# Attention and SwiGLU on one core: where the casts of wo stand behind the exponentials, and which places the last projected rows use

## The chip, the cores and the metric

The kernel runs on one core of a Trainium2 chip. The metric is the device time of one execution in microseconds; the time before is the median of three runs. A profiled execution, whose instructions are quoted below, is a run of its own with a time of its own.

## The reference, cut to what matters

```python
S, D, H, Dh, F = 2048, 576, 32, 18, 4608

def A(x, wqkv, w_phi, wo):                    # linear attention with a learned feature map
    q, k, v = heads_of(x @ wqkv)              # 32 heads of 18 columns
    pq, pk = q @ w_phi, k @ w_phi             # per head
    phi_q = concat(softmax(pq), softmax(-pq)) # over the 18 columns of a head
    phi_k = concat(softmax(pk), softmax(-pk))
    kv, z = phi_k^T v, sum_s phi_k            # per head
    o = (phi_q kv) / (phi_q z + 1e-6)
    return o @ wo

def B(x, w_gate, w_up, w_down):
    return (silu(x @ w_gate) * (x @ w_up)) @ w_down

xn = layernorm(x)
out = x + A(xn) * silu(B(xn))
```

All inputs and the output are float32.

## The kernel before, in words

Products are made at float32 accuracy from parts. A helper `split(hi, lo, src)` casts a tile to TensorE's own 32-bit format on ACT (line 58) and subtracts the cast from the source on DVE (line 59); a product is then three matmuls of the parts. `split_rows` (lines 62 to 64) does the same for the weights of the early gate and up tiles.

The program has these stages, in order of time.

1. Layer norm, transposes, and the folding of the feature map into the weights of k and q (to about 100 us).
2. k and v: 16 tiles of 128 rows, and the sums kv and z (to about 230 us).
3. q and the projection (about 230 to 480 us): 16 tiles of 128 rows, two at a time. `q_tile` multiplies the rows by the folded weights into a PSUM tile of one place (`p2`, two banks; in the trace its matmuls write `p`). `softmax_parts` reads that tile on DVE four times (lines 278 and 279, a maximum and a subtraction, then a minimum and a subtraction, into the SBUF tile `e`), then makes two exponentials on ACT in place (line 282) and sums them by heads on DVE (`sm`, line 285). What follows of `q_tile` on DVE is the denominator: `ez` is `e` times z (line 567), `y` its sums (line 569), five small operations (lines 571 to 576), and `e` times the result (line 577). `numer` transposes `e` of a pair of tiles on TensorE (line 588), splits, and multiplies by kv (line 594). `project` multiplies by the parts `WOH` and `WOL` of wo (line 614); ACT copies each half of 128 x 288 out of PSUM into an SBUF tile `so` (line 619), and ACT's own DMA queue stores it (line 620).
4. gate, up and down with Strassen's scheme, two passes of 1024 rows (about 513 us to the end). `gate_up_weights` loads weights into `ld`, makes sums on GpSimd (POOL, lines 694 to 697), splits them into `w`, and stores the parts in DRAM for the second pass. Its first call stands before the loop over the units.

Between and beside stages 2 to 4, "early" tiles of gate and up (`early_tile`) run as plain products: a gate product into a PSUM tile `pe` (two places), a silu of it on ACT into `h` (line 119), an up product into the other place, and a multiplication on DVE (line 122). Their weights come through `raw` in `early_weights`.

`tails(n)` prepares tails of the gate and up weights: a load into `tl`, four POOL subtractions (lines 546 to 549), a cast into `th` on ACT (line 550), a DVE subtraction, and twelve stores that POOL issues.

wo comes in five groups of rows, two groups to a tile: `wrs` lists three tiles, which take the places of `oh`, `ol` and, for the last group, `ez`. `split_wo`, called after the second of the first two q tiles, splits them into `WOH` and `WOL`.

What sets the order: a scheduler places each engine's instructions at compile time, by priority (the order of the program, unless a block is under `tc.high_priority()`) among those that its own times hold ready; each engine then runs its list in that order. `with tc.issue_after(ins)` puts the block's instructions that run on the engine of `ins` behind `ins` in that engine's list, and no others. A pool's tile name with `bufs=n` has n places; a tile that finds none free waits for the release of the oldest. `read` lists the DVE subtractions of `softmax_parts`, so `read[-1]` is a DVE instruction.

Of the kernel before, what the change touches and what calls it, by code (L numbers as in the profile page):

```python
# [9 lines left out]
F32 = mybir.dt.float32  # L10
F32R = mybir.dt.float32r
AF = mybir.ActivationFunctionType
# [4 lines left out]
S, D, H, DH, F = 2048, 576, 32, 18, 4608  # L17
P = 128
# [5 lines left out]
HALF = D // 2  # L24
# [13 lines left out]
def heads(ap):  # L38
    return ap.rearrange("p (h d) -> p h d", d=DH)
# [7 lines left out]
def gated_hedgehog_kernel(ctx: ExitStack, tc, x, w_qk, w_v, w_phi, wo, w_gu, w_tail, w_down, ident_in, mask_in, out):  # L47
# [5 lines left out]
    nc = tc.nc  # L53
# [3 lines left out]
    def split(hi, lo, src):  # L57
        nc.scalar.copy(hi, src)  # L58
        nc.vector.tensor_sub(lo, src, hi)  # L59
# [53 lines left out]
    def early_tile(f, i, parts, js=(0, 1), banks=None):  # L113
        for j in js:
            pg, pu = banks or [eps.tile([P, BT], F32, name="pe") for _ in range(2)]
            xw(pg, i, j, slice(0, BT), *parts[0], False)
            h = epool.tile([P, BT], F32, name="h")
            with tc.high_priority():
                nc.scalar.activation(h, pg, AF.Silu)  # L119
            last = xw(pu, i, j, slice(0, BT), *parts[1], False)  # L120
            with tc.high_priority():
                nc.vector.tensor_mul(h, pu, h)
            nc.sync.dma_start(h_dram[i, f, :, j * BT:(j + 1) * BT], h)
        return last

    with ExitStack() as att:
        const = att.enter_context(tc.tile_pool(name="const", bufs=1))
        ident = const.tile([P, P], F32, name="ident")
# [7 lines left out]
        with ExitStack() as wst:  # L136
# [129 lines left out]
            kk = kst.enter_context(tc.tile_pool(name="kk", bufs=2, side="right", reuse_waits="tile"))  # L266
# [6 lines left out]
            def softmax_parts(ps, e):  # L273
                m = kk_pool.tile([P, 2, H], F32, name="m", bufs=1)
                p4 = ps[:, :, 0:HALF].rearrange("p a (h d) -> p a h d", d=DH)
                for s, op in enumerate((ALU.max, ALU.min)):
                    m3 = m[:, s].rearrange("p (a h) -> p a h", a=2)
                    nc.vector.tensor_reduce(m3, p4, axis=AX.X, op=op)
                    read.append(nc.vector.tensor_sub(e[:, s * D:(s + 1) * D].rearrange("p (a h d) -> p a h d", a=2, d=DH),
                                                     p4, m3.unsqueeze(3).to_broadcast([P, 2, H // 2, DH])))  # L280
                for s in range(2):
                    nc.scalar.activation(e[:, s * D:(s + 1) * D], e[:, s * D:(s + 1) * D], AF.Exp,
                                         scale=1.0 if s == 0 else -1.0)
                sm = kk_pool.tile([P, 2 * H], F32, name="sm")
                nc.vector.reduce_sum(sm, heads(e), axis=AX.X)
                return sm

            kk_pool, read = kk, []

            def kv_step(n, phi, v):  # L290
                for i in range(2 * NG):
# [108 lines left out]
            def k_tile(t):  # L400
                i0, j0, cols = block(t)
                pk = kps.tile([P, 2, 512], F32, name="p2")
                for i in range(2):
                    w = slice(i * HALF, (i + 1) * HALF)
                    xw(pk[:, i, 0:HALF], i0, j0, cols, KVWH[:, :, :, w], KVWL[:, :, :, w], True)
                phi = kk.tile([P, 2 * D], F32, name="phi", bufs=2)
                sm = softmax_parts(pk, phi)
                nc.vector.reciprocal(sm, sm)
                nc.vector.tensor_mul(heads(phi), heads(phi), spread(sm, 2 * H))
                return phi  # L410
# [111 lines left out]
        with ExitStack() as qst:  # L522
            qw = qst.enter_context(tc.tile_pool(name="qw", bufs=1, reuse_waits="tile"))
            qk = qst.enter_context(tc.tile_pool(name="qk", bufs=2, reuse_waits="tile"))
# [1 line left out]
            WOH = qw.tile([GW, NG, D], F32R, name="WOH")  # L526
            WOL = qw.tile([GW, NG, D], F32R, name="WOL")
            wrs = [qk.tile([P, 2, D], F32, name="oh", bufs=1), qk.tile([P, 2, D], F32, name="ol", bufs=1),
                   qk.tile([P, 2, D], F32, name="ez", bufs=1)]
            for g, (o, w) in enumerate(GROUPS):  # L530
                nc.sync.dma_start(wrs[g // 2][0:w, g % 2], wo[o:o + w, :])

            def split_wo():
                with tc.issue_after(read[-1].ins):
                    for n, wr in enumerate(wrs):
                        g, w = slice(2 * n, min(2 * n + 2, NG)), GROUPS[2 * n][1]
                        split(WOH[0:w, g], WOL[0:w, g], wr[0:w, 0:min(2, NG - 2 * n)])

            kk_pool = qk
# [58 lines left out]
            def project(b, oh, ol, last):  # L598
                for j in range(QS // P):
                    pair = qps.tile([P, 2, 512], F32, name="p2") if last and j == 0 else None  # L600
                    jc = slice(j * P, (j + 1) * P)
                    r0 = b * QS + j * P
                    for i in range(2):
                        n = slice(i * HALF, (i + 1) * HALF)
                        if pair:
                            ps = pair[:, i]
                        elif last and i:
                            ps = qps.tile([P, 2, 512], F32, name="p2")[:, 0]
                        else:
                            ps = qps.tile([P, 512], F32, name="p")  # L610
                        k = 0
                        for g, (o, w) in enumerate(GROUPS):
                            for a, bw in ((oh, WOH), (oh, WOL), (ol, WOH)):
                                nc.tensor.matmul(ps[:, 0:HALF], a[0:w, g, jc], bw[0:w, g, n], start=k == 0,  # L614
                                                 stop=k == 3 * NG - 1)
                                k += 1
                        so = qk.tile([P, HALF], F32, name="so", bufs=2)
                        with tc.high_priority() if last else ExitStack():
                            nc.scalar.copy(so, ps[:, 0:HALF])
                        nc.scalar.dma_start(s_dram[r0:r0 + P, n], so)  # L620

            order = list(range(S // QS // 2, S // QS)) + list(range(S // QS // 2))
# [1 line left out]
            for n in range(S // QS + 1):  # L624
                new = []
                if n > 0:
                    om = numer(es)
                if n < S // QS:
                    new += [q_tile(order[n] * (QS // P) + j) for j in range(QS // P)]
                if n == 0:  # L630
                    split_wo()
                if n > 0:
                    project(order[n - 1], *om, n == S // QS)
                es = new
# [34 lines left out]
    def gate_up_weights(i, f):  # L669

        parts, wt = {}, fw.tile([96, 7, P], F32R, name="wt", bufs=2)
        n, q = divmod(f - EARLY, 4)
        if i == 0:
            ld = fw.tile([P, 2, D], F32, name="ld", bufs=2).rearrange("p a b -> p (a b)")
            ld = ld[:, 0:8 * P].rearrange("p (m c n) -> p m c n", m=4, c=2)
            nc.sync.dma_start(ld, w_gu[f, :, :, 0:2])
            ts = fw.tile([P, D], F32, name="ts")[:, 0:4 * P].rearrange("p (m c n) -> p m c n", m=2, c=2)

        def ready(m, src):
            k = 1 if m == 6 else 2  # L680
            w = fw.tile([P, k, 4, P], F32R, name=f"w{k}", bufs=2 if k == 1 else 4)
            if i:
                nc.sync.dma_start(w.bitcast(F32), w_dram[f - EARLY, :, m:m + k])
            else:
                split(w[:, :, 0:2], w[:, :, 2:4], src)
                if f < NF - 1:
                    nc.sync.dma_start(w_dram[f - EARLY, :, m:m + k], w.bitcast(F32))
            for c in range(k):
                parts[m + c] = w[:, c]

        ready(0, None if i else ld[:, 0:2])
        nc.sync.dma_start(wt.bitcast(F32), t_dram[n, q].rearrange("b r m n -> (b r) m n"))
        if i == 0:
            nc.gpsimd.tensor_sub(ts[:, 0], ld[:, 2], ld[:, 0])
            nc.gpsimd.tensor_sub(ts[:, 1], ld[:, 3], ts[:, 0])
            nc.gpsimd.tensor_sub(ld[:, 2], ld[:, 3], ld[:, 2])
            nc.gpsimd.tensor_sub(ld[:, 1], ld[:, 1], ts[:, 1])  # L697
        ready(4, None if i else ts)
        ready(2, None if i else ld[:, 2:4])
        ready(6, None if i else ld[:, 1:2])  # L700
        return parts, wt
# [319 lines left out]
    todo = [(i, f) for i, n, f in units if f >= EARLY and (i == 0 or f < NF - 1)]  # L1021
# [5 lines left out]
        nc.sync.dma_start(t, w_down[f * P:(f + 1) * P, :])  # L1027
    xo = operands(0)
    early_tile(EARLY - 1, 0, parts)
    ready = [gate_up_weights(*todo.pop(0))]  # L1030
    est.close()
    fq = ctx.enter_context(tc.tile_pool(name="fq", bufs=1, reuse_waits="tile"))
    fps = ctx.enter_context(tc.tile_pool(name="fps", bufs=1, space=PSUM, reuse_waits="tile"))
# [72 lines left out]
```

## Time and profile before

| | |
|---|---|
| Median of three runs | 1636.75 us (1635.69, 1636.75, 1640.77) |
| Profiled execution, its own time | 1638.38 us |
| Its span, first to last instruction | 1636.6 us |
| TensorE (PE) busy | 1604.0 us, 98% |
| DVE busy | 1168.5 us, 71% |
| ACT busy | 721.9 us, 44% |
| POOL busy | 653.3 us, 40% |
| Granted TensorE clock, mean | 0.998 of full speed |

PE is the matmul, PEld TensorE's loading of weights, which overlaps it; SP issues most DMAs. In a timeline a row is: start in us from the start of the span, duration in us, engine, line, operation, output tile and input tiles, shape, count, and in brackets the idle time of that engine just before with what ended it. In a table of waits a row is: who waited, for what, total us, times, longest us. Consecutive instructions of one engine overlap a little, so a row can start before the row ahead of it has ended.

### The profile page before, as it was taken

The numbers are of one execution on the slowest core, as the hardware profiler recorded it, in microseconds if no ns is written. First come the engines' busy times: TensorE is split into PE (matmuls) and PEld (weight loads), VectorE is DVE, ScalarE is ACT, GpSimd is POOL, SyncE is SP. The second block draws the span as 40 slices with busy tenths as digits, with TensorE's granted clock in tenths as the row PEclk, the third lists the DMA queues.
The fourth block names the chain that finished last, engine by engine and source line by source line (L and its number), as shares of the span: only waits on it lengthen the run. The fifth ranks groups of instructions, "written<-read, shape, count | busy, mean of one in ns | idle before, by whom it ended". The sixth has DMA issues, their size and how long they took to land.

```text
span 1636.6 us, 25198 instructions
## 1 busy us (share of the span) xinstructions
PE 1604.0 (98%) x9385; PEld 1429.7 (87%) x9385; DVE 1168.5 (71%) x1721; ACT 721.9 (44%) x1391; POOL 653.3 (40%) x699
## 2 busy tenths in 40 slices
PE   6999998999999999999999999999999999999998
PEld 5899997999978888888888888888888888888887
DVE  7677768899952678778777778825666766666578
ACT  5533345444432554544444544455433433333334
POOL 3485661333212455455545355313233324133132
PEclk9999999999999999999999999999999999999999
DMA  9622243334248545555554554684454655555444
GB/s 286 206 80 78 85 134 117 117 103 126 67 144 306 184 165 175 179 178 168 177 180 165 175 192 152 224 296 150 136 162 135 199 184 170 172 179 185 140 115 174
DMA packets 121741, 268.46 MB, mean 164 GB/s; under 512 B 12787, under 2 KB 53363, under 8 KB 119827
## 3 DMA queue, kind: packets, MB, share of 16 engines
q1 hardware_dynamic: 106652, 246.49, 45.9%
q0 software_dynamic: 3072, 11.02, 2.4%
q10 hardware_dynamic: 11894, 9.35, 1.8%
q8 instruction: 74, 1.21, 0.3%
q14 instruction: 49, 0.39, 0.1%
HBM read 167.19 MB, written 99.61 MB: 163 GB/s over the span
## 4 chain that ended last, share of the span: by engine, by line
PE 90%; DMA 4%; DVE 3%; POOL 1%; issue 1%; ACT 1%; SPq 0%; ACTq 0%; POOLq 0%; DVEq 0%
PE px L707 24%; PE pd L832 24%; PE pw L707 12%; PE py L707 6%; PE p L92 6%; PE pe L92 5%; PE p L614 4%; PE po L594 2%; PE kvp L294 2%; PE vx L382 1%; PE pt L588 1%; DMA xn<-in_A_x 1%; PE vw L382 1%; DMA s_dram<-so 1%; DMA sraw<-in_A_w_v 1%
## 5 line engine op out<-in xcount | busy, mean ns | idle before, releaser
L832 PEld LDWEIGHTS pd<-dw,hh 128*128 128x128 f32 x3048 | 432.4, 188 | 26.4 <-DVE dw L59 1.7
L832 PE MATMUL pd<-dw,hh 128*128 128x288 f32 x3048 | 448.5, 297 | 4.3 <-DVE dw L59 1.5
L707 PE MATMUL px<-X,w 128*128 128x512 f32 x1488 | 384.3, 393 | 0.0
L707 PEld LDWEIGHTS px<-X,w 128*128 128x128 f32 x1488 | 270.6, 188 | 51.8 <-ACT s L736 2.0
L707 PE MATMUL pw<-X,w 128*128 128x512 f32 x732 | 188.7, 393 | 0.0
L707 PEld LDWEIGHTS pw<-X,w 128*128 128x128 f32 x732 | 137.0, 188 | 30.5
L741 DVE TENSOR_TENSOR s<-pw,s 128x512 f32<-128x512 f32 x124 | 85.1, 688 | 100.0 <-ACT s L736 89.2
L957 DVE TENSOR_TENSOR acc<-pd,acc 128x576 f32<-128x576 f32 x128 | 96.2, 752 | 83.8 <-PE pd L832 83.6
L736 ACT COPY s<-px 128x512 f32<-128x512 f32 x124 | 72.6, 585 | 157.2 <-PE px L707 157.2
L92 PE MATMUL pe<-X,wh 128*128 128x512 f32 (+1 forms) x380 | 121.8, 401 | 5.8 <-ACT h L119 2.9
L59 DVE TENSOR_TENSOR hh<-ha,hh 128x512 fp32r<-128x512 f32 x140 | 111.5, 823 | 20.7 <-ACT hh L58 19.1
L58 ACT CAST hh<-ha 128x512 fp32r<-128x512 f32 x140 | 82.7, 619 | 92.4 <-PE pd L832 73.5
L929 POOL TENSOR_TENSOR hb<-hb 128x512 f32<-128x512 f32 x34 | 47.0, 1381 | 168.6 <-DVE hb L753 161.4
L59 DVE TENSOR_TENSOR w<-ld,w 128x512 fp32r<-128x512 f32 (+1 forms) x93 | 77.2, 832 | 35.7 <-ACT w L58 34.5
L707 PE MATMUL px<-X,wt 96*128 96x512 f32 x248 | 97.9, 395 | 0.0
L707 PE MATMUL py<-X,w 128*128 128x512 f32 x372 | 96.5, 394 | 0.0
L916 POOL TENSOR_TENSOR h<-ha,hb 128x512 f32<-128x512 f32 x34 | 44.3, 1302 | 126.8 <-DVE ha L757 88.6
L942 POOL TENSOR_TENSOR ha<-ha 128x512 f32<-128x512 f32 x34 | 52.6, 1564 | 103.5 <-DVE hh L59 103.5
L58 ACT CAST w<-ld 128x512 fp32r<-128x512 f32 (+1 forms) x93 | 51.0, 549 | 89.6 <-POOL ld L697 56.8
L92 PEld LDWEIGHTS pe<-X,wh 128*128 128x128 f32 (+1 forms) x380 | 70.0, 189 | 21.7 <-ACT h L119 3.4
L761 ACT COPY py<-px 128x512 f32<-128x512 f32 x62 | 35.5, 572 | 102.7 <-PE px L707 80.8
L707 PEld LDWEIGHTS py<-X,w 128*128 128x128 f32 x372 | 66.7, 188 | 11.2
(262 smaller groups left out, 3199.0 us busy)
## 6 DMA issues: line engine op xcount, KB each, us to landing
w_dram<-w SPq DMA_DIRECT2D x90, 512.0 KB, 2.9
w<-w_dram SPq DMA_DIRECT2D x90, 512.0 KB, 4.5
wt<-t_dram SPq DMA_DIRECT2D x61, 336.0 KB, 3.7
ld<-in_B_w_gu SPq DMA_DIRECT2D x31, 512.0 KB, 4.5
X<-sum_dram SPq DMA_DIRECT2D x8, 1280.0 KB, 11.1
rt<-in_B_w_down SPq DMA_DIRECT2D x33, 288.0 KB, 3.1
rb<-in_B_w_down SPq DMA_DIRECT2D x33, 288.0 KB, 4.7
w_dram<-w SPq DMA_DIRECT2D x30, 256.0 KB, 2.1
```

Source lines behind the costliest of these rows:

```text
L58: nc.scalar.copy(hi, src)
L59: nc.vector.tensor_sub(lo, src, hi)
L92: last = nc.tensor.matmul(ps, l, r, start=n == 0, stop=n == len(pairs) - 1)
L614: nc.tensor.matmul(ps[:, 0:HALF], a[0:w, g, jc], bw[0:w, g, n], start=k == 0, stop=k == 3 * NG - 1)
L707: nc.tensor.matmul(ps, l, r, start=first and n == 0, stop=last and n == len(mm) - 1, skip_group_check=True)
L736: nc.scalar.copy(t, ps)
L741: nc.vector.tensor_add(t, ps, t)
L832: nc.tensor.matmul(ps, l, r, start=first and n == 0 and m == 0, stop=n == len(hs) - 1 and m == 2, skip_group_check=True)
L916: sub(s, g["h"][0][0], g["h"][0][1])
L929: nc.gpsimd.tensor_add(a21, a21, g["h"][1][1])
L942: sub(a12, a12, g["h"][0][0])
L957: nc.vector.tensor_add(a2, pd[:, :, 0:HALF], a2)
```

## The change

- In `softmax_parts` the exponentials are recorded in a new list `exps`. `split_wo` puts its block behind `exps[-1]`, the second exponential of the second q tile, on ACT, instead of behind `read[-1]`, that tile's last subtraction, on DVE.
- The third of the `wrs` tiles takes one of the four places of `e` instead of the one place of `ez`.
- In the last call of `project`, the second half of each row block (`i` = 1) is copied into a place of `e` instead of `so`. All output copies are recorded in a list `outs`.
- The first call of `gate_up_weights` puts its ACT instructions behind `outs[-1]`, the last output copy.

```diff
+    outs = []
...
                 for s in range(2):
-                    nc.scalar.activation(e[:, s * D:(s + 1) * D], e[:, s * D:(s + 1) * D], AF.Exp,
-                                         scale=1.0 if s == 0 else -1.0)
+                    last = nc.scalar.activation(e[:, s * D:(s + 1) * D], e[:, s * D:(s + 1) * D], AF.Exp,
+                                                scale=1.0 if s == 0 else -1.0)
+                exps.append(last)
...
-            kk_pool, read = kk, []
+            kk_pool, read, exps = kk, [], []
...
             wrs = [qk.tile([P, 2, D], F32, name="oh", bufs=1), qk.tile([P, 2, D], F32, name="ol", bufs=1),
-                   qk.tile([P, 2, D], F32, name="ez", bufs=1)]
+                   qk.tile([P, 2 * D], F32, name="e", bufs=4).rearrange("p (a n) -> p a n", a=2)]
...
             def split_wo():
-                with tc.issue_after(read[-1].ins):
+                with tc.issue_after(exps[-1].ins):
...
-                        so = qk.tile([P, HALF], F32, name="so", bufs=2)
+                        if last and i:
+                            so = qk.tile([P, 2 * D], F32, name="e", bufs=4)[:, 0:HALF]
+                        else:
+                            so = qk.tile([P, HALF], F32, name="so", bufs=2)
                         with tc.high_priority() if last else ExitStack():
-                            nc.scalar.copy(so, ps[:, 0:HALF])
+                            outs.append(nc.scalar.copy(so, ps[:, 0:HALF]))
                         nc.scalar.dma_start(s_dram[r0:r0 + P, n], so)
...
-    ready = [gate_up_weights(*todo.pop(0))]
+    with tc.issue_after(outs[-1].ins):
+        ready = [gate_up_weights(*todo.pop(0))]
```

## The prediction

> **What bounds the kernel now.** I read the page's busy times first, then the table of TensorE's waits over the span, then the timelines of PE, ACT and DVE around the two places that the change touches.
>
> ```profile
> PE 1604.0 (98%) x9385; PEld 1429.7 (87%) x9385; DVE 1168.5 (71%) x1721; ACT 721.9 (44%) x1391; POOL 653.3 (40%) x699
> PE tp L193 <- DVE xn L181: 11.4, 2, 10.4
> ```
>
> TensorE is busy for 98% of the span. The change removes no matmul, so it can only give back time in which PE stands still, and 11.4 us of that lie at the start, before anything that the change touches. Around the two places PE stands still six times:
>
> ```profile
> 247.53 0.29 PE L92 MATMUL p<-QH,X 128*128 128x288 f32 x1
> ...
> 255.40 0.50 PE L92 MATMUL pe<-X,wh 128*128 128x512 f32 x1 [1.19 <-ACT h L119]
> 260.49 0.50 PE L92 MATMUL pe<-X,wh 128*128 128x512 f32 x1 [1.55 <-DVE h L122]
> 270.36 0.37 PE L92 MATMUL p<-QH,X 128*128 128x288 f32 x1 [1.42 <-DVE e L279]
> ...
> 477.94 0.40 PE L614 MATMUL p<-WOH,oh 126*128 126x288 f32 x1 [1.17 <-ACT so L619]
> 485.39 0.50 PE L92 MATMUL pe<-X,wh 128*128 128x512 f32 x1 [0.28 <-ACT h L119]
> 489.57 0.47 PE L92 MATMUL pe<-X,wh 128*128 128x512 f32 x1 [0.63 <-ACT h L119]
> ```
>
> The brackets add up to 1.19 + 1.55 + 1.42 = 4.16 us in the first place and 1.17 + 0.28 + 0.63 = 2.08 us in the second: 6.24 us together, the most that the change can return directly. A measurement of this kernel can tell about 0.3%, 4.9 us, from no change, so nearly all of it has to come back before the change counts as faster.
>
> Why PE waits in the first place is seen on ACT and DVE, from the first q tile's exponentials on:
>
> ```profile
> 239.61 1.26 ACT L282 ACTIVATE e<-e 128x576 f32<-128x576 f32 x2
> 244.86 1.16 ACT L58 CAST WOH<-oh 126x1152 fp32r<-126x1152 f32 x1 [3.99 <-DMA oh<-in_A_wo]
> 248.05 1.16 ACT L58 CAST WOH<-ol 126x1152 fp32r<-126x1152 f32 x1 [2.04 <-DMA ol<-in_A_wo]
> 249.12 0.66 ACT L58 CAST WOH<-ez 72x576 fp32r<-72x576 f32 x1
> 251.19 0.94 ACT L550 CAST th<-tl 128x896 fp32r<-128x896 f32 x1 [1.41 <-POOL tl L549]
> 252.04 0.68 ACT L282 ACTIVATE e<-e 128x576 f32<-128x576 f32 x1
> ...
> 253.46 1.28 ACT L119 ACT_TABLE_LOAD   x1
> 254.75 0.60 ACT L119 ACTIVATE h<-pe 128x512 f32<-128x512 f32 x1
> 255.37 1.28 ACT L282 ACT_TABLE_LOAD   x1
> 256.66 0.69 ACT L282 ACTIVATE e<-e 128x576 f32<-128x576 f32 x1
> 257.36 1.28 ACT L119 ACT_TABLE_LOAD   x1
> 258.98 0.60 ACT L119 ACTIVATE h<-pe 128x512 f32<-128x512 f32 x1 [0.33 <-PE pe L92]
> ```
>
> ```profile
> 243.00 1.35 DVE L285 TENSOR_REDUCE sm<-e 128x64 f32<-128x1152 f32 x1
> 244.27 0.75 DVE L278 TENSOR_REDUCE m<-p 128x32 f32<-128x576 f32 x1
> ...
> 246.51 0.76 DVE L279 TENSOR_TENSOR e<-p,m 128x576 f32<-128x576 f32 x1
> 247.19 1.35 DVE L59 TENSOR_TENSOR WOL<-oh,WOH 126x1152 fp32r<-126x1152 f32 x1
> 253.47 0.69 DVE L63 TENSOR_TENSOR wl<-raw,wh 128x512 fp32r<-128x512 f32 x1 [4.94 <-ACT wh L62]
> ...
> 255.90 0.75 DVE L59 TENSOR_TENSOR WOL<-ez,WOH 72x576 fp32r<-72x576 f32 x1
> 257.24 1.34 DVE L567 TENSOR_TENSOR ez<-e,zb 128x1152 f32<-128x1152 f32 x1
> 259.76 0.68 DVE L122 TENSOR_TENSOR h<-pe,h 128x512 f32<-128x512 f32 x1
> 269.46 0.75 DVE L279 TENSOR_TENSOR e<-p,m 128x576 f32<-128x576 f32 x1
> ```
>
> ACT stands with the casts of wo at the head of its list, waiting for their DMAs (3.99 and 2.04 us), then with `th` waiting for POOL (1.41 us). The second q tile's numbers are subtracted by 246.51 + 0.76 = 247.27, yet its exponentials start at 252.04 and 256.66. DVE therefore idles 4.94 us before 253.47, while even the first tile's `ez`, whose exponentials ended at 240.87, cannot run: its only place holds the last wo rows until their subtraction (255.90). It comes at 257.24. From 253.47 on DVE works off a queue, and two of PE's waits, 1.55 and 1.42, are for operations in it (259.76 and 269.46).
>
> In the second place ACT waits twice:
>
> ```profile
> 473.36 0.40 ACT L619 COPY so<-p 128x288 f32<-128x288 f32 x1 [1.02 <-PE p L614]
> 476.97 0.62 ACT L58 CAST w<-ld 128x512 fp32r<-128x512 f32 x1 [3.22 <-DMA ld<-in_B_w_gu]
> 477.50 0.39 ACT L619 COPY so<-p 128x288 f32<-128x288 f32 x1
> 481.18 0.40 ACT L619 COPY so<-p 128x288 f32<-128x288 f32 x1 [3.29 <-DMA s_dram<-so]
> 483.92 0.40 ACT L619 COPY so<-p 128x288 f32<-128x288 f32 x1 [0.26 <-DMA s_dram<-so]
> 484.74 0.60 ACT L119 ACTIVATE h<-pe 128x512 f32<-128x512 f32 x1
> ```
>
> The second of the last four copies stands behind a cast of `w` that waits 3.22 us for its load, and PE waits for the bank that it frees. The third waits 3.29 us for the first one's store, because there are two `so` places; the silu at 484.74, for which PE waits 0.28, stands behind it.
>
> **The change part by part.**
>
> *Casts of wo behind the second tile's exponentials.* Nothing is added; three casts (1.16 + 1.16 + 0.66 = 2.98 us on ACT) and their subtractions move. The exponentials can run from 247.27, and the casts follow with their DMAs landed: 247.3 + 1.4 + 3.0 = 251.7 for the end of them, about where `th` stands now. WOL is read first at 277.0, so the casts have 20 us of cover:
>
> ```profile
> L614 PE MATMUL p<-WOL,oh x160: 289/294/299, 277.0 to 479.8; 126*128 126x288 f32 x128, 72*128 72x288 f32 x32
> L707 PE MATMUL px<-X,w x36: 389/393/405, 512.8 to 528.5; 128*128 128x512 f32 x36
> ```
>
> Queued behind the casts on ACT are `th`, `wh` and the silu of 254.75. One exponential (0.68) no longer lies ahead of that silu, so of the 1.19 us wait I take 0.6; bounds: all 1.19, or a loss of 2.98 if the casts, instead of the idle time, stand ahead of it. With both exponentials together, two table loads (255.37 and 257.36, 2 x 1.28 us) should also go; the waits that follow belong to DVE, so I give that nothing. [...]
>
> *The last wo rows in an `e` place.* Four places, of which the first three q tiles take three and the fourth the freed one; its load is the same. `ez` of the first tile can now run once DVE reaches it, in the idle 4.94 us. DVE then stands nearly 5 us earlier in its queue, and PE's two waits on it add up to 2.97: I take both, 1.55 + 1.42. Bounds: 0, if the hole stays closed, and 2.97. What is late next would be the silu on ACT. First place: 0.6 + 2.97 = 3.57 us.
>
> *Output copies first, two in `e` places.* The `e` places are those of q tiles that `numer` has long transposed, so none of the four copies has a store to wait for. The second copy, at 477.50, can follow the first, at 473.76: the 1.17 goes. The silu is no longer behind copies that wait: the 0.28 goes. Of the 0.63 I take half, 0.3, since the wait is for a second `pe` place too, which a multiplication on DVE frees, and DVE's list there holds subtractions of weights. Second place: 1.75 us; bounds 1.17 and 2.08.
>
> *First gate and up weights behind the last copy.* The new wait: casts of `w` stand behind a copy whose product, fifteen matmuls of at most 0.3 us, starts at 477.94 - 1.17 = 476.8 and ends by 481.3. Four casts of at most 0.62 us end by 483.8, before the silu of today (484.74). Behind them wait POOL's sum into `ld`, SP's stores of `w`, and the loads of `w_down` rows that SP issues after; the first product reads `w` at 512.8, 29 us later. Cost nothing; without that cover, up to the 4.3 us by which the first cast (476.97) moves.
>
> *Sum.* 3.57 + 1.75 = 5.3 us. The profiled execution, 1638.38, would be 1633.1; its time stands 1.6 above the median of the three runs, so the median goes from 1636.75 to 1631.4, 0.32% faster.
>
> **The rivals.**
>
> *`th` takes the casts' place at the head of ACT's list.* The scheduler put `th` ahead of the second tile's exponentials, by its own times, although it comes later in the program; with the casts held back, it has no reason to put it later. ACT then stands until POOL is done (251.19) and the exponentials run at 252.04 and 256.66 as now. The casts follow at 257.35 and end at 260.33; the silu of 258.98 slides to there, and PE's wait at 260.49 grows: 260.33 + 0.60 + 0.68 = 261.6, 1.1 us later. DVE still does the first tile's work in its hole, so the 1.42 goes. Net 0.3, with the second place 2.0 us: 1634.7, no change that can be told. For it speaks the position of `th` today; against it, that `th` was placed when ACT had the casts as company. [...]
>
> *The first tile's denominator goes ahead of the second tile's reads.* `ez` comes earlier in the program than the second tile's maximum (244.27), and it is no longer held. What one tile has from `ez` on takes DVE 5.5 us without a break:
>
> ```profile
> 453.87 1.35 DVE L567 TENSOR_TENSOR ez<-e,zb 128x1152 f32<-128x1152 f32 x1
> ...
> 458.00 1.36 DVE L577 TENSOR_TENSOR e<-e,y 128x1152 f32<-128x1152 f32 x1
> ```
>
> (458.00 + 1.36 - 453.87 = 5.49.) Placed after `sm` (243.00), it moves the reads, and with them PE's next q tile, which needs their bank, from 247.53 to 253.0; the exponentials follow, and then 2.98 us of casts ahead of a silu. If PE's list has nothing in front, it loses 5.5 + 3.0 = 8.5; it gains 1.75 at the end and the 1.42. Net 5.3 slower: 1642.0. It decides from a loss of 8.1 us on (4.9 + 3.2); any early product of 3 us that PE takes in between brings it back to no change. The priorities speak for it; PE's supply of early products speaks against the full price.
>
> *The change doesn't act*: the order is as before, 1636.8.
>
> **How the numbers follow.** Forecast 42%, `th` 36%, the denominator ahead 20%, no effect 2%. So faster by over 0.3%: 0.42; within: 0.38; slower: 0.20. The low end takes all 6.24 us and the 1.1 by which the lowest of the three runs lies under the median: 1629.4. The high end is the slower rival, 1642.0; the range between holds both signs, and the forecast's own range is 1629.4 to 1632.0 (the second place at 1.17 instead of 1.75).
>
> **What would show it.** Right: on ACT both exponentials of the second tile before the first WOH cast and close to 248, no table load between them; on DVE `ez` before 253 and no idle time near 5 us ahead of `wl`; PE without the waits of 1.55 and 1.42; four `so` copies with no DMA in their brackets, and no L614 wait for `so`. Wrong: `th` ahead of the exponentials with a POOL wait of several us; a PE wait for `e` L279 near 247; or new PE waits after 513, where the order of the rest may have shifted.

## The result, and the profile after

The changed kernel takes 1643.63 us (median of 6 runs, 1641.54 to 1645.53); the kernel before, in runs beside it, 1638.09 us. The ratio is 1.0034, with a 95% interval of 1.002 to 1.0047: slower by 0.34%, where 1631.4 us, 0.32% faster, was forecast, and above the range's high end of 1642.0. The profiled execution of after took 1641.54 us, the lowest of the six, span 1639.4. Lines below 126 keep their numbers; in `softmax_parts` they grow by 1, behind it by 2, from the output copies on by 5.

The table of TensorE's waits over the span, after:

```profile
PE tp L194 <- DVE xn L182: 12.1, 2, 10.7
PE px L712 <- ACT s L741: 4.9, 2, 3.8
PE p L92 <- DVE e L280: 2.9, 2, 1.6
```

The waits of the second place are gone from it, and one is new: px for `s`, 4.9 us. The same on PE's timeline, around the two places and at the entry of the loop over the units:

```profile
241.60 0.47 PE L92 MATMUL pe<-X,wh 128*128 128x512 f32 x1 [0.70 <-DVE h L122]
243.72 0.58 PE L92 MATMUL p<-QH,X 128*128 128x288 f32 x1 [1.65 <-DVE e L280]
256.60 0.37 PE L92 MATMUL p<-QH,X 128*128 128x288 f32 x1 [1.23 <-DVE e L280]
...
530.18 1.65 PE L712 MATMUL px<-X,w 128*128 128x512 f32 x6 [1.10 <-ACT s L741]
539.63 1.33 PE L837 MATMUL pd<-dw,hh 128*128 128x288 f32 x8 [0.58 <-DVE dw L59]
549.55 2.14 PE L712 MATMUL px<-X,w 128*128 128x512 f32 x6 [3.76 <-ACT s L741]
```

Busy times by stretch of 25 us, PE's first (of 25.00) and the granted clock third from the end, before:

```profile
225.00:250.00 25.00, 25.00 (x162) 22.86 (x161) 16.37 (x22) 11.26 (x18) 12.97 (x15) 1.00 0.64 207
250.00:275.00 25.00, 20.84 (x107) 16.91 (x106) 21.18 (x33) 16.24 (x19) 6.87 (x15) 1.00 0.39 123
475.00:500.00 25.00, 22.93 (x107) 18.21 (x106) 8.05 (x11) 6.50 (x13) 9.72 (x11) 1.00 0.90 311
...
525.00:550.00 25.00, 22.39 (x108) 18.42 (x107) 15.86 (x23) 13.43 (x26) 13.25 (x13) 1.00 0.64 226
550.00:575.00 25.00, 25.00 (x144) 22.36 (x143) 16.71 (x26) 15.21 (x30) 11.46 (x12) 1.00 0.58 193
```

and after:

```profile
225.00:250.00 25.00, 22.65 (x136) 20.36 (x135) 14.37 (x20) 8.48 (x15) 13.49 (x17) 0.93 0.65 211
250.00:275.00 25.00, 23.77 (x123) 19.98 (x122) 22.72 (x35) 15.97 (x20) 6.69 (x15) 1.00 0.41 122
475.00:500.00 25.00, 25.00 (x137) 20.90 (x136) 7.88 (x14) 7.08 (x16) 8.24 (x10) 1.00 0.65 208
...
525.00:550.00 25.00, 19.56 (x93) 15.91 (x92) 17.20 (x20) 11.45 (x24) 16.26 (x18) 1.00 0.68 223
550.00:575.00 25.00, 25.00 (x128) 21.88 (x127) 16.49 (x25) 14.20 (x29) 10.92 (x11) 0.93 0.59 200
```

First place (225 to 275): idle 4.16 us before, 2.35 + 1.23 = 3.58 after, a gain of 0.58. Second place (475 to 500): 2.07 before, 0 after. Entry of the loop (525 to 550): 2.61 before, 5.44 after. The three nearly cancel (+0.18 us). What doesn't cancel are the two 0.93 in the clock's column. Fine windows over those two stretches show what they are (length, PE busy, clock):

```profile
239.89:243.30 3.41, 1.48 (x6) 1.00 0.83 258
243.30:246.71 3.41, 2.99 (x12) 0.50 0.85 257
...
547.09:550.50 3.41, 0.95 (x4) 1.00 0.48 189
550.50:553.91 3.41, 3.41 (x14) 0.50 0.96 296
```

TensorE ran at half clock (0.50 granted) for one stretch of 3.41 us behind the waits of 1.65 and of 3.76 us. In the first stretch the 12 matmuls into `p` from 243.72 on took 3.01 us; the same 12 took 1.66 us, from 243.54 to 245.20, in abc_no_hold (below) at a granted clock of 1.00. From these figures I estimate that a stretch costs half of what PE does in it, up to 1.7 us. Over the runs (123 of before, 6 of after) the mean granted clock was 0.9977 before and 0.9955 after; over 1637 us that is 3.6 us by my estimate (1637 x 0.0022), most of what the medians differ by. So in the profiled run the change moved waits about, for nothing in sum, and two of the new ones were followed by half clock.

**Where the wait for `s` comes from.** SP's timeline at the loop's entry, before:

```profile
514.20 0.33 SPq L890 DMA_DIRECT2D rt<-in_B_w_down  x1
...
515.55 0.43 SPq L890 DMA_DIRECT2D rb<-in_B_w_down  x1
```

and after:

```profile
512.33 7.42 SPq L692 DMA_DIRECT2D w_dram<-w  x7
...
523.29 0.33 SPq L895 DMA_DIRECT2D rt<-in_B_w_down  x1
526.73 6.56 SPq L692 DMA_DIRECT2D w_dram<-w  x4
533.34 0.44 SPq L895 DMA_DIRECT2D rb<-in_B_w_down  x1
...
536.34 0.61 SPq L895 DMA_DIRECT2D rt<-in_B_w_down  x1
...
551.17 0.74 SPq L895 DMA_DIRECT2D rb<-in_B_w_down  x1
```

The first four loads of `w_down` rows stood together, ahead of the loop's first loads; now stores of `w` stand between them. POOL, after, and then ACT:

```profile
539.22 1.02 POOL L922 TENSOR_TENSOR td<-rb,rt 128x288 f32<-128x288 f32 x1
...
542.63 0.95 POOL L699 TENSOR_TENSOR ts<-ld 128x256 f32<-128x256 f32 x1
...
544.69 0.72 POOL L701 TENSOR_TENSOR ld<-ld 128x256 f32<-128x256 f32 x1
545.38 0.79 POOL L929 TENSOR_TENSOR td<-td,rb 128x288 f32<-128x288 f32 x1
```

```profile
546.21 0.43 ACT L58 CAST dw<-td 128x288 fp32r<-128x288 f32 x1 [4.98 <-POOL td L929]
...
548.91 0.58 ACT L741 COPY s<-px 128x512 f32<-128x512 f32 x1
```

Before, POOL made the row sum `td` (L917 there) at 518.81. After, it comes 20 us later; behind it come two more row sums and three sums of weights, and only then the `td` of L929 for which ACT has waited 4.98 us with a cast at its head. The snapshot `s`, which frees PE's px bank, stands behind that cast; PE goes on at 549.55.

**In the first place**, DVE after:

```profile
234.19 0.75 DVE L279 TENSOR_REDUCE m<-p 128x32 f32<-128x576 f32 x1
240.76 0.69 DVE L122 TENSOR_TENSOR h<-pe,h 128x512 f32<-128x512 f32 x1 [5.83 <-issue]
241.37 0.75 DVE L280 TENSOR_TENSOR e<-p,m 128x576 f32<-128x576 f32 x1
...
252.85 0.69 DVE L63 TENSOR_TENSOR wl<-raw,wh 128x512 fp32r<-128x512 f32 x1 [1.75 <-ACT wh L62]
...
254.11 0.75 DVE L280 TENSOR_TENSOR e<-p,m 128x576 f32<-128x576 f32 x1
```

An early product's multiplication stands ahead of the first tile's read of `p2` (before, both subtractions of that tile were done by 236.73), hence PE's 0.70 and 1.65. The second tile's subtraction stands behind `wl` and the first tile's denominator, at 254.11 instead of 246.51.

### The profile page after: what moved, and what is told of

The parts are those of the page before. It is cut to its first block, busy times and chain, and to the rows that moved or that the text cites. A ratio compares the mean times of both kernels' runs of the same rounds, so it can differ in the third digit from the quotient of the medians.

```text
span 1639.4 us, 25196 instructions
## 1 busy us (share of the span) xinstructions
PE 1605.6 (98%) x9385; PEld 1431.6 (87%) x9385; DVE 1171.4 (71%) x1721; ACT 721.7 (44%) x1391; POOL 656.0 (40%) x699
## 4 chain that ended last, share of the span: by engine, by line
PE 65%; DVE 1%; DMA 0%; issue 0%; ACT 0%; ACTq 0%; DVEq 0%; SPq 0%
PE pd L837 24%; PE px L712 24%; PE pw L712 12%; PE py L712 6%; DVE acc L809 0%; DMA X<-s_dram 0%; DVE hh L59 0%; DVE acc L810 0%; DVE s L746 0%; DVE acc L994 0%; DVE ha L762 0%; ACT w L58 0%; DVE w L59 0%; DVE X L962 0%; DVE acc L962 0%
```

## The experiments

The theories at the start were: the loss lies at the loop's entry, through the late rows (theory 1); it lies in the first place, through the read of `p2` behind a multiplication (theory 2); it is only clock and noise (theory 3). Each kernel was timed in 10 to 12 runs (after in 6) beside runs of before on the same chip, whose medians were 1638.1 to 1638.95. "Clock" is the mean over the runs of the granted clock (before: 0.9977); "idle" and "half" are PE's idle time and the stretches of 3.41 us at half clock between 225 and 600 us in the one profiled run (before: 8.86 us, none).

| kernel | median us | ratio, 95% interval | clock | idle | half |
|---|---|---|---|---|---|
| the change (after) | 1643.63 | 1.0034 [1.002, 1.0047] | 0.9955 | 9.05 | 2 |
| f2_rows_first | 1639.29 | 1.0003 [0.9993, 1.0014] | 0.9967 | 5.31 | 1 |
| abc_no_hold | 1640.78 | 1.001 [1.0, 1.002] | 0.9961 | 9.41 | 1 |
| acd_ez_place | 1637.08 | 0.9994 [0.9986, 1.0003] | 0.9976 | 5.85 | 0 |
| cd_second_only | 1638.32 | 0.9996 [0.9986, 1.0006] | 0.9977 | 6.48 | 2 |
| late_rows | 1641.42 | 1.0017 [1.0009, 1.0026] | 0.9969 | 9.29 | 2 |
| acd_rows_first | 1637.45 | 0.999 [0.9979, 1.0] | 0.9976 | 6.60 | 1 |
| acd_rows_th | 1636.58 | 0.999 [0.9981, 1.0] | 0.9972 | 7.25 | 1 |
| cd_rows_first | 1637.59 | 0.9992 [0.9983, 1.0001] | 0.9980 | 7.48 | 1 |
| a_alone | 1642.16 | 1.0014 [1.0005, 1.0023] | 0.9971 | 8.24 | 0 |
| b_alone | 1643.49 | 1.0027 [1.0018, 1.0036] | 0.9959 | 8.30 | 1 |
| c_alone | 1640.72 | 1.0009 [1.0, 1.0018] | 0.9971 | 8.79 | 2 |
| ac_rows_th | 1639.23 | 1.0003 [0.9994, 1.0012] | 0.9976 | 7.23 | 1 |
| f2_read_first | 1639.47 | 1.0011 [1.0001, 1.0021] | 0.9960 | 7.31 | 4 |
| f2_read_th | 1639.58 | 1.0006 [0.9997, 1.0015] | 0.9960 | 7.61 | 2 |

The four parts of the change are called A (casts of wo behind the exponentials), B (last wo rows in an `e` place), C (last copies in `e` places) and D (the hold on the first gate and up weights).

**The rows first.** The whole change, and

```diff
         t = fq.tile([P, D], F32, name=name, bufs=2)
-        nc.sync.dma_start(t, w_down[f * P:(f + 1) * P, :])
+        with tc.high_priority():
+            nc.sync.dma_start(t, w_down[f * P:(f + 1) * P, :])
```

> The changed kernel with one thing added: the loads of w_down rows for stage 4 stand under high priority, so that SP issues the first four of them ahead of the stores of w and of the loop's first loads, as before the change. Theory 1, the loss lies at the entry of the loop (SP has the rows of w_down behind the stores of w, so POOL's sums of them, the casts on ACT and the snapshot of the px bank come late): PE's waits for s of 3.76 and 1.10 us go, the clock in 550 to 560 is back at 1.00, and the time falls by 4 to 6 us against the changed kernel, to 1637 to 1639, at or a little below the kernel before. Theory 2, the loss lies in the first place (the first tile's read of p2 behind an early product's multiplication): no more than 1 us changes. Theory 3, the loss is nothing but clock and noise: no change, and the waits for s stay or go without the time following.

1639.29 us, 4.3 under the change (5.1 by the two ratios to before). SP issued the four loads at 516.20 to 518.63, POOL's sums ran at 521.89 to 524.46, and no wait for `s` is left: between 525 and 575 PE waits only

```profile
541.67 0.53 PE L837 MATMUL pd<-dw,hh 128*128 128x288 f32 x2 [0.31 <-DVE hh L59]
544.60 1.35 PE L837 MATMUL pd<-dw,hh 128*128 128x288 f32 x8 [1.25 <-DVE dw L59]
```

The clock is 1.00 there. Theory 1 holds for most of the loss, with a fall at the low end of the 4 to 6 us; the time is before's, so the gain of the second place is still given back somewhere. The edit moved other loads of SP's list too (the fourth load of `ld` stands at 527.52 here, at 533.88 in after), so the fall isn't shown to be the rows' alone.

**The rows late, alone.** The kernel before, and

```diff
+        late = [11, 11, 11, 11]
-        nc.sync.dma_start(t, w_down[f * P:(f + 1) * P, :])
+        with tc.issue_after(wst[late[k]].ins) if k < 4 else ExitStack():
+            nc.sync.dma_start(t, w_down[f * P:(f + 1) * P, :])
```

(`wst` lists the stores of `w`, `k` counts the loads).

> The kernel before with one thing changed: SP issues the first four loads of w_down rows behind the twelfth store of w, some 13 to 25 us later than before; nothing else of the change is made. Theory 1 (the rows, late on SP, are what makes the loop's entry lose): PE waits for s at L740 by 2 to 5 us in all near 530 to 550, where before had no such wait, the mean clock over the runs falls by 0.001 or more, and the time rises by 3 to 6 us, to 1642 to 1645. Rival: the late rows are harmless by themselves and the waits for s came from elsewhere in the change (the casts of w behind the copies, the order of ACT's list): the time stays within 1 us of before.

1641.42 us, 2.6 above the runs of before beside it: the rival falls, and the expected size was too large. The wait that grew is another one than I named:

```profile
542.13 0.53 PE L832 MATMUL pd<-dw,hh 128*128 128x288 f32 x2 [2.24 <-DVE hh L59]
544.17 2.29 PE L832 MATMUL pd<-dw,hh 128*128 128x288 f32 x8 [1.50 <-DVE dw L59]
```

POOL's three row sums, now at 534.50 to 537.06, push its sum of `h` from 538.21 to 540.16, and 1.10 becomes 2.24. Here POOL makes the row sums ahead of that `h`, ACT's cast of `td` waits 1.54 us, and px doesn't wait for `s`. In the kernel before, late rows cost by themselves; the 3.76 of after needs that kernel's POOL list too, in which the sums stand behind `h` (537.52).

**Three of the four parts.** Without B:

> The change without the e place: the last wo rows stay in the place of ez. DVE's list then has both reads of the first tile ahead of the early product's multiplication, as before. Theory 2: PE's waits of 0.70 and 1.65 us and the clock of 0.93 near 240 to 250 go, and the time is 3 us under the changed kernel or more. Theory 1: SP's list here still has two of the first four rows of w_down behind the loop's first loads, so most of the waits for s stay; against the changed kernel 2 us at most from the first place, little from the loop: 1640 to 1643.

Without D:

> The change without the hold on the first gate and up weights: their casts stand in ACT's list where the scheduler puts them, among the last copies. Theory 1: the stores of w come some 20 us earlier on SP, so the rows of w_down come earlier too (two of the first four still stand behind the loop's first loads), and PE's 3.76 us wait for s shrinks by half or more: 1638 to 1641, while one copy again stands behind a cast that waits for its load (up to 1.17 us). Theory 2: the first place keeps its loss; no faster than the changed kernel, 1643 to 1645.

C and D alone:

> The second place's half of the change alone: last output copies in e places, and the first gate and up weights behind the last copy; the casts of wo and the place of the last wo rows as before. In SP's list the rows of w_down stay ahead of the loop's first loads. Theory 1: the loop's entry is as before, the second place gives its 2 us: 1634.5 to 1636.5 beside 1638 of before. Theory 2: the same, since the first place is untouched. If it is slower than before, the waiting casts of w alone cost time, and both are wrong.

Without B the time is 1637.08, 6.5 under the change: more than theory 1 gave, and as theory 2 had it. Without D it is 1640.78, in the range that theory 1 gave, but the wait for `s`, which it had shrinking, stays at 3.89: the hold isn't what makes the rows late (first load at 520.09, fourth at 545.23), it only adds to it. Nor do the rows make that wait here. The three row sums were done at 533.18, and what stands ahead of `s` is a load of `ld`, on POOL and, through its sums, on ACT:

```profile
538.49 0.74 POOL L699 TENSOR_TENSOR ts<-ld 128x256 f32<-128x256 f32 x1 [1.79 <-DMA ld<-in_B_w_gu]
...
543.97 0.41 ACT L58 CAST w<-ld 128x256 fp32r<-128x256 f32 x1 [2.37 <-POOL ld L702]
```

Without B the rows are as late (518.36 to 543.11), and PE waits 1.54 us for `s`.

C and D alone, 1638.32, miss the expected 1634.5 to 1636.5: their idle time is 2.4 under before's, and two half-clock stretches (259.75 and 543.06) were in the profiled run, though not in the mean of the clock. At this size the start of the kernel blurs a profiled run: PE's idle time up to 225 us, which no part touches, was 16.0 to 19.1 us.

**The e place with the rows early.** Against f2_rows_first this differs by B alone:

> The change without the e place for the last wo rows, and with the rows of w_down first on SP. Against f2_rows_first it differs by the e place alone. Theory 2 in its clock form (the e place puts two waits, 0.70 and 1.65 us, within 3 us, and TensorE then often runs at half clock for 3.4 us): the mean clock rises from 0.9967 to 0.9975 or more, and the time falls by 1.5 to 2.5 us, to about 1637. If the e place costs nothing, it stays at 1639. Against acd_ez_place it differs by the rows alone: one wait for s of 1.5 us goes, 1 us or less.

1637.45 us and a clock of 0.9976: 1.8 under f2_rows_first, as theory 2 in its clock form said, though the two intervals overlap. Against acd_ez_place, which has the rows late, nothing is gained (1637.45 and 1637.08). So the two losses don't add up: with B the rows' place is worth 4.3 us, without it nothing that can be told; B costs 6.5 us with the rows late and 1.8 with them early.

**th off ACT's head.** acd_rows_first, and

```diff
-                nc.scalar.copy(hi, t)
+                with tc.issue_after(exps[NT + 1].ins):
+                    nc.scalar.copy(hi, t)
```

> As acd_rows_first, and the cast into th put behind the second q tile's exponentials on ACT, so that it can't take ACT's head. If th at the head costs what it did in the rival of the prediction (the exponentials start 4 to 5 us late, then PE waits for the silu and the multiplication), PE's waits between 250 and 275 fall from 3.8 us to 2 or less and the time is 1.5 to 2 us under acd_rows_first. If those waits belong to something else (the product before them, POOL), the time stays.

PE's idle time at 250 to 275 is 2.80 us (3.01 in acd_rows_first), and 0.9 us in the medians isn't told from nothing. ACT shows why:

```profile
247.49 0.69 ACT L283 ACTIVATE e<-e 128x576 f32<-128x576 f32 x1 [4.98 <-DVE e L280]
252.79 0.83 ACT L62 CAST wh<-raw 128x768 fp32r<-128x768 f32 x1 [4.62 <-DMA raw<-in_B_w_gu]
...
254.93 0.60 ACT L119 ACTIVATE h<-pe 128x512 f32<-128x512 f32 x1
```

The exponential now starts at 247.49, where the prediction wanted it, and little comes of it: the next cast waits until 252.79 for the early weights, and the silu behind it starts at 254.93 (254.77 in acd_rows_first). This run is 1.73 us later from the first tile's maximum on (235.34 against 233.61), so in its place the silu is 1.6 us earlier, and PE's wait of 1.30 for it is gone. But the wait of 1.70 for the multiplication stays, and one of 1.11 for a q tile's subtraction is new.

**C and D, and the parts by themselves.**

C and D with the rows first:

> The second place's half of the change with the rows of w_down first on SP: the casts of wo and their places as before. Theory 1: the 1.0 us wait for s of cd_second_only goes and no other comes; 1636.5 to 1638. If the hold on the casts behind the exponentials is worth something by itself, acd_rows_first is faster than this by 1 us or more; if not, the two agree within 1 us.

A alone:

> The casts of wo behind the second tile's exponentials, and nothing else of the change. In SP's list the first two rows of w_down stay early, the other two come behind the loop's first loads. If the first place is worth next to nothing (th takes ACT's head, so PE's waits between 250 and 275 stay near 4 us), and two late rows cost half of what four do: 1639 to 1641 beside 1638.8 of before. By the prediction's sum for this part (0.6 us of the silu's wait, the table loads for nothing): 1638.2.

B alone:

> The last wo rows in a place of e, and nothing else of the change. In DVE's list the early product's multiplication stands ahead of the first tile's read, and in SP's list the first row of w_down is early, the others come behind the loop's first loads. If the place alone brings both losses (0.70 + 1.65 us close together at 240 to 245 with half-clock stretches behind them, and late rows): 1641 to 1643, nearly as slow as the whole change. By the prediction's sum for this part (2.97 us of DVE's queue): 1635.9.

C alone:

> The last output copies in places of e, and nothing else of the change: the first casts of w stand among the copies as before, and no list of DVE, ACT or SP is reordered elsewhere. The waits for a store behind the copies go, the one copy behind a cast of w that waits for its load stays (up to 1.17 us): 1637.5 to 1638.8. Against cd_second_only (1638.3 beside 1638.95 of before) it shows what the hold on the first gate and up weights is worth: by the prediction about 1 us.

acd_rows_th without D:

> The parts that the runs so far leave standing: casts of wo behind the exponentials, last copies in places of e, th behind the exponentials, the rows of w_down first on SP; no e place for the wo rows, no hold on the first weights. Against acd_rows_th (1636.6) it differs by the hold. If the hold makes the loop's entry lose (its waits of 1.7 for s and 1.6 for hh against none and 1.1 in before), this is 1 to 2 us faster, 1634.5 to 1636; if the hold is worth the 1 us of the prediction in the second place, it is 1 us slower, 1637.5.

cd_rows_first, 1637.59, agrees with acd_rows_first (1637.45): A is worth nothing here. Its 1.0 us wait for `s` (521.07) stayed, against the expectation.

B alone is nearly the whole loss, 1643.49, 4.6 above before beside it, with both waits in the first place and one for `s`. PE's timeline:

```profile
241.85 0.47 PE L92 MATMUL pe<-X,wh 128*128 128x512 f32 x1 [0.70 <-DVE h L122]
243.97 0.58 PE L92 MATMUL p<-QH,X 128*128 128x288 f32 x1 [1.65 <-DVE e L279]
...
549.16 1.66 PE L707 MATMUL px<-X,w 128*128 128x512 f32 x6 [3.48 <-ACT s L736]
```

As in abc_no_hold, the row sums were done long before that last wait (at 535.7).

A alone and C alone are slower than expected, 1642.16 and 1640.72. A's profiled run was the fastest of its eleven, so its trace doesn't show where the rest goes; that stays open. C alone keeps the copy behind a waiting cast (1.31 us). The hold D is worth 2.4 us against C alone (1638.32) and 2.7 in the last pair (1636.58 beside 1639.23), by the ratios 2.1 each, with intervals that overlap; that is more than the prediction gave it. With B in, it cost 2.9 (1640.78 to 1643.63).

**One instruction of DVE.** f2_rows_first, and the early product's multiplication behind the first tile's second subtraction:

```diff
-            with tc.high_priority():
+            with tc.high_priority(), tc.issue_after(behind.ins) if behind else ExitStack():
                 nc.vector.tensor_mul(h, pu, h)
```

(`behind` is `read[2 * NT + 1]` for that one product). f2_read_th adds the edit of acd_rows_th.

> As f2_rows_first (the whole change, and the rows of w_down first on SP), with one DVE instruction moved: the early product's multiplication (L122) that stood between the first q tile's maximum and its subtraction stands behind that tile's second subtraction. Theory 2 (this one place in DVE's list makes the e place cost 1.6 us): PE's waits of 0.70 and 1.65 us near 242 to 246 go, the mean clock rises from 0.9967 to 0.9975, and the time falls from 1639.3 to 1637 to 1637.7, as without the e place. Rival (the subtraction waits for its own place in memory, so DVE only waits there instead): the waits stay or grow, and so does the time, 1639 to 1640.

> As f2_read_first, and the cast into th behind the second tile's exponentials. With th off ACT's head the exponentials of the second tile follow DVE's subtractions at once. If that is worth anything with the e place (where ez of the first tile stands ahead of the second tile's reads on DVE), 0.5 to 1.5 us under f2_read_first, 1636 to 1637; if DVE's list sets those waits, no difference.

1639.47 and 1639.58: theory 2 in this form falls, and so does its rival. The 0.70 and 1.65 are gone, the subtractions ran at 236.85 and 238.31 without a wait, and PE stands later instead:

```profile
257.13 0.79 PE L92 MATMUL pe<-X,wh 128*128 128x512 f32 x1 [4.34 <-ACT h L119]
```

With `th` moved, ACT's cast before that silu waits 10.98 us for `raw` (to 252.95) and PE 4.15. So with `th` moved the first place is set by the arrival of the early weights. With `th` at the head it is set by POOL's tails, for which `th` waits (to 251.19 before, to 251.02 after); the cast `wh` behind it then finds its load landed. The two come about a microsecond apart: counted from the first tile's maximum, the silu starts 21.0 us later in before, 19.9 in after, 19.6 in acd_rows_th, 20.4 in f2_read_first and 20.3 in f2_read_th, whatever ACT had ahead of it. PE arrives there earlier or later; its idle time from 225 to 275 is 1.7 to 4.6 us in all these kernels. SP issues these loads (from 244.39 before, 245.27 after) behind those of wo and `tl`; an order with the early weights first wasn't tried.

## Why the prediction was wrong

*Second place: right.* 1.75 us were forecast, 2.07 of PE's idle time came back in the profiled run. In the times it hardly shows: C and D alone, which make it, are 0.6 us under before, inside the noise. The four copies follow PE at 482.70 to 488.23 without a store in their brackets, the casts of `w` start at 488.52, later than the 483.8 that I had them end by, since `project` itself came later.

*"The last wo rows in an `e` place ... I take both, 1.55 + 1.42": the step that failed most.* The sum took 2.97 us faster for it. By itself it makes the kernel 4.6 us slower (b_alone), and the change without it is 6.5 us faster (acd_ez_place). The term counted what the freed place lets DVE run and put the order of all other work at nothing. In after, b_alone and abc_no_hold, DVE's list has an early product's multiplication ahead of the first tile's read, SP's list has its loads in another order, PE waits 3.48 to 3.89 us for `s`, and the mean clock is lower (0.9955 to 0.9961, before 0.9977). "Where the order of the rest may have shifted" stood among the signs of a wrong forecast, unpriced. How the 4.6 us divide among the first place, the loop's entry and the clock isn't settled: pinning the rows takes back 4.3 of the change, moving the multiplication nothing.

*"DVE then stands nearly 5 us earlier in its queue"; and 0.6 of the silu's wait.* Instead of 3.57 us, 0.58 of idle time went. The hole of 4.94 us ended with `wl <- ACT wh L62`, and I took the late exponentials for its cause. acd_rows_th has the first of them at 247.49, and the hole is there still (4.75 us before `wl` at 253.65). There the chain was the load of `raw`, then `wh`; with `th` in front it was POOL's tails, then `th`, then `wh`.

*"Cost nothing" for the first gate and up weights.* The list of what is queued behind the held casts was right, and held the loads of `w_down` rows; the cover was read for one of them only, the first reader of `w` at 512.8. The rows' reader, POOL's sums for the products `pd`, was never looked up. Late rows alone cost 2.6 us (late_rows), and the hold costs 2.9 with B in; without B it looks like a gain. The hold isn't the main cause of the lateness: without it the rows are late all the same, and with B alone too.

*The rivals.* `th` did take ACT's head (251.02, after 6.73 us), as the second case had it, but that decided nothing. And the first tile's `ez` and sums did go ahead of the second tile's subtraction (254.11), as the third case had it, at a price of one PE wait of 1.23 us, not 5.5. That the time landed near that case's 1642.0 is luck: it came by another road.

*The clock.* All waits were priced at their own length. The two half-clock stretches of the profiled run, and 3.6 us in the mean over the runs, were in no term.

## What to carry to other kernels

When an edit holds instructions back, list every DMA and sum queued behind them and look up the first reader of each, not only of the tile in view; where a scheduler builds the lists, a change of one tile's place can reorder loads on another engine, so compare all lists, and pin the order of loads that matter (one line gave 4.3 us in the changed kernel). Before an idle stretch is counted as a gain, follow what ends it back to a DMA: in acd_rows_th, where the arrival of `raw` ended it (252.79), the exponential moved ahead to 247.49 gained 0.9 us in the medians, which isn't told from nothing. The versions without B and with C and D are the lowest here (acd_rows_th 1636.58, ratio 0.999 [0.9981, 1.0]: about a tenth of a per cent under before).

## What the runs showed of the clock

The half-clock stretches are 3.41 us long or twice that (late_rows, from 542.8 to 549.7). In the profiled run of after they sit on a grid: they start at 18.02, 243.30 and 550.50, which is 225.28 and 307.20 us apart, 66 and 90 times 3.4133 us. Below, a run is cut into windows of that length, counted to within 0.1 us from a half-clock stretch of its own (at 261.08 in acd_rows_first, 548.76 in abc_no_hold, 243.56 in b_alone). The windows ahead of a stretch at half clock had PE busy for 1.48 and 0.95 us (after, shown above), and in acd_rows_first

```profile
257.60:261.01 3.41, 1.70 (x7) 1.00 0.43 174
261.01:264.42 3.41, 3.41 (x10) 0.51 0.21 77
```

while in abc_no_hold, whose grid lies otherwise against the same waits of 0.70 and 1.65 us (the first ends 0.1 us ahead of a window's start, in after 1.7 us behind one), this one was followed by full clock:

```profile
241.52:244.93 3.41, 1.76 (x11) 1.00 0.88 267
```

and b_alone, whose wait of 3.48 us for `s` fell on two windows, kept full clock, in both and behind them:

```profile
543.93:547.34 3.41, 1.75 (x13) 1.00 0.35 94
547.34:550.75 3.41, 1.58 (x7) 1.00 0.62 241
```

Of the windows shown, those with 0.95, 1.48 and 1.70 us busy were followed by half clock, those with 1.58, 1.75 and 1.76 by full: they show no sharp border. The waits of 0.70 and 1.65 us led to half clock in after and not in abc_no_hold; that this hangs on how the grid falls is my reading, which no run shows by itself. The clock shows in the 123 runs of before, too: mean clocks of 0.999, 0.998, 0.997 and 0.996 go with mean times of 1637.2, 1638.4, 1640.0 and 1641.6 us, 1.2 to 1.6 us for each step, about one stretch by the estimate of up to 1.7 us.
